# Attention and MLP on one core: last whole weight pieces decoded into PSUM, unit 3 finished ahead of unit 4, step 14's product ahead of step 16

## The chip, the core and the metric

The kernel runs on one core of a Trainium2 chip. The metric is the device time of one execution in microseconds. Its engines work side by side, each through its own queue in order: TensorE (PE, and PEld for its weight loads), VectorE (DVE), ScalarE (ACT), GpSimd (POOL) and SyncE (SP, which issues DMAs). The kernel's program text is ordered by a scheduler in its first part and by hand afterwards, as told below.

## The reference

Attention over 8 batches, 8 heads, 576 positions and 64 elements a head, in fp32, and an MLP on its 4608 x 512 result:

```python
q_d = q.reshape(B, H, Sd, factor, D).mean(axis=3)
...
out_d = sm_attn(q_d, k_d, v_d)
out_up = np.repeat(out_d, factor, axis=2)
mask = np.abs(pos[:, None] - pos[None, :]) < factor
scores = scale * np.matmul(q, k.transpose(0, 1, 3, 2))
scores = np.where(mask, scores, -1000000000.0)
...
out_local = np.matmul(attn, v)
return (out_up + out_local).astype(np.float32)
...
h = x @ w_in
g = np.maximum(h, 0.0) + alpha * np.minimum(h, 0.0)
return (g @ w_out).astype(np.float32)
```

So there is a full attention over 144 averaged positions (factor 4), a local one over seven neighbours, their sum x, and then x (512) to 2048 hidden elements and back to 512.

## The kernel before

**The MLP and its steps.** The 4608 tokens are 18 chunks of 256. A chunk takes 8 steps (NP), each for 256 of the hidden elements, so there are 144 steps. For step s, `hidden` (L771) computes h by 24 matmuls; `slopes` (L782 to L786, ACT) makes the two products whose maximum is the activation; `larger` (L794, DVE, from step EARLY = 12; POOL before) takes the maximum t; `split` (ACT L799, POOL L72) writes t as gh plus gl; `product` (L828) adds 12 matmuls into the chunk's output tiles o; after a chunk's last step `finish` (L834, ACT) copies o out and SP sends it. Each fp32 operand is split in a high and a low part, and a product is high by high, high by low and low by high: xh with wih and wil, xl with wih; gh with woh and wol, gl with woh.

**The weights.** They come as raw fp32 words and are decoded on the chip by `make` (L174 to L226): magnitude (ACT L196), reach (DVE L200, L201), bits (DVE L205, L206), upper (ACT L211 or L215, writes wih or woh) and lower (DVE L219 or L223, writes wil or wol). Pieces fp = 0 to 4 of each matrix are done whole, 1024 elements in each partition, in a ring of two SBUF buffers (temp); pieces 5 to 7 in blocks of 512 in two PSUM banks, "q" and "l".

**The attention.** `down` computes the averaged attention of two heads (qkT L264, s L277, dnb L281, pT L301, pv L311, od L316). `local` computes the local one in units of 192 tokens, three a batch: unit u's scores by a multiply (qk, L608) and a reduction (ls, L612) for three groups of neighbours and two halves, a softmax (L621 to L638), the weighted sums (first L660, weigh L664, gather L667 into the accumulator lb; the far neighbours on POOL, L644), and last (L670), which writes x. PE then transposes x (`flip`, L676, tile xp), DVE adds the averaged attention (`join`, L688, tile xf), and `place` splits xf in xh (ACT L702) and xl (POOL L72). Chunk 2 (steps 16 to 23) needs unit 3's two joins, xf3_0 and xf3_1; chunk 3 (steps 24 to 31) needs unit 4 and the first part of unit 5. Until the chunk's xh and xl are there, its first step can't run.

**What sets the order.** Every piece is an event with a time in steps: `hidden` of step s at s - 1.95, `product` at s + 0.6; a unit's pieces are spread from begin[u] to begin[u + 1], where UNITS gives the first ones; its flips and joins stand at times relative to the next unit's (`before 0`, `before 1`, `own`). The events are sorted. Those before time LISTED = 14 are handed to a scheduler that may reorder them on each engine; those from 14 on are taken as listed (L983 to L990). An engine's queue runs in order, so a row that waits holds up all behind it.

Buffers that matter: both joins of a unit write the one "xf" buffer, which steps before 12 also use for sh; the multiplies of a unit use two "prod" buffers; there are two "pp" buffers for POOL's far products. The banks "q" and "l" hold the decode's blocks, and later a unit's scaled q (qp) and its accumulator.

## Time and profile before

| what | value |
|---|---|
| median of 3 runs | 986.85 us (985.21 to 992.86) |
| the profiled execution | 989.45 us, of which its span 987.6 us |
| busy, share of the span: PE / DVE / ACT / POOL | 96% / 84% / 56% / 51% |
| TensorE's mean granted clock | 0.977 |
| 190 to 204 us: PE busy, clock | 7.64 of 14.00 us, 0.63 |
| 204 to 252 us: PE busy, DVE busy | 47.34 and 43.00 of 48.00 us |
| 600 to 700 us: PE busy, DVE busy | 99.81 and 91.10 of 100 us |

Rows of the timeline give start, duration, engine, line, operation and operands (out<-in), the tile shape and a count of rows taken together; a bracket is the idle time of the engine just before, with the row that ended it. Matmuls overlap at their ends, so a row's start-to-start distance, and not its duration, is its price. Groups of rows add a mean in ns.

### The profile page before, as it was taken

Reading aid. Unit: us, or ns where it says so; the run is one execution under the profiler, and the core shown is the slowest. Engines: PE = TensorE matmul, PEld = TensorE weight load, DVE = VectorE, ACT = ScalarE, POOL = GpSimd, SP = SyncE. Lnnn points to the kernel's source line nnn. Section 1 sums busy time; section 2 is a strip of 40 time slices with the busy share of each in tenths; the row PEclk is TensorE's granted clock in tenths of the full one; section 3 lists DMA queues with packets and bytes.
Section 4 is the critical chain, followed back from the end, with each engine's and each line's share of the span. In section 5 each row is a group of like instructions: output and inputs, shape, how many; then the busy total and the mean of one; then the engine's idle time right before and its main releaser. Section 6 shows DMA issues by size and latency. Waiting matters only on the chain.

```text
span 987.6 us, 17973 instructions
## 1 busy us (share of the span) xinstructions
PE 944.3 (96%) x6402; PEld 844.3 (85%) x6402; DVE 826.4 (84%) x1336; ACT 557.4 (56%) x1483; POOL 508.2 (51%) x624
## 2 busy tenths in 40 slices
PE   5977999799999999999999999999999999999998
PEld 4856887599889998889988899998899989989997
DVE  7799978989888898998989889899898889997111
ACT  4667676355656564655555555555646564444442
POOL 2063886557566545655546455555466633323221
PEclk9966999899999999999999999999999999999999
DMA  8935743123433323242312332322333311310000
GB/s 200 229 136 174 251 131 108 55 81 97 129 112 101 94 84 100 88 138 73 127 59 93 102 121 72 122 79 84 115 102 99 119 47 56 102 33 22 1 22 22
DMA packets 63197, 98.28 MB, mean 100 GB/s; under 512 B 23556, under 2 KB 28932, under 8 KB 63108
## 3 DMA queue, kind: packets, MB, share of 16 engines
q1 hardware_dynamic: 62916, 96.88, 32.5%
q8 instruction: 50, 0.82, 0.3%
q10 hardware_dynamic: 192, 0.26, 0.1%
q14 instruction: 39, 0.32, 0.1%
HBM read 87.67 MB, written 9.44 MB: 98 GB/s over the span
## 4 chain that ended last, share of the span: by engine, by line
PE 81%; DVE 12%; ACT 2%; issue 2%; SPq 1%; POOL 1%; DMA 1%; DVEq 0%; ACTq 0%; POOLq 0%
PE o L828 36%; PE h L771 36%; PE s L277 2%; PE pv L311 2%; PE xp L676 1%; DVE lb L667 1%; PE pT L301 1%; DVE temp L205 1%; DVE temp L206 1%; DVE pv L664 1%; PE fs L462 1%; DVE qk L608 1%; SPq L410 1%; DVE temp L200 1%; DVE wil L219 1%
## 5 line engine op out<-in xcount | busy, mean ns | idle before, releaser
L72 POOL TENSOR_TENSOR gl<-t,gh 128x512 fp32r<-128x512 f32 x144 | 186.3, 1293 | 344.4 <-ACT gh L799 330.9
L782 ACT ACTIVATE t<-h,slope 128x256 f32<-128x256 f32 x288 | 136.4, 474 | 136.1 <-PE h L771 106.4
L771 PE MATMUL h<-xh,wih 128*128 128x256 f32 x1152 | 188.4, 285 | 9.1 <-ACT xh L702 3.5
L828 PE MATMUL o<-woh,gh 128*128 128x512 f32 x576 | 192.5, 404 | 2.7 <-ACT gh L799 1.2
L828 PE MATMUL o<-wol,gh 128*128 128x512 f32 x576 | 185.7, 393 | 0.0
L828 PE MATMUL o<-woh,gl 128*128 128x512 f32 x576 | 185.4, 393 | 0.0
L771 PE MATMUL h<-xl,wih 128*128 128x256 f32 x1152 | 180.2, 279 | 0.9 <-POOL xl L72 0.9
L771 PEld LDWEIGHTS h<-xh,wih 128*128 128x128 f32 x1152 | 163.3, 190 | 20.5 <-ACT sh L784 3.8
L771 PE MATMUL h<-xh,wil 128*128 128x256 f32 x1152 | 180.6, 279 | 0.0
L794 DVE TENSOR_TENSOR t<-h,t 128x512 f32<-128x512 f32 x132 | 90.6, 686 | 94.7 <-ACT h L786 92.2
L75 POOL TENSOR_TENSOR ld<-ld 72x256 f32<-72x256 f32 x168 | 132.5, 791 | 68.2 <-DMA ld<-in_q 64.8
L799 ACT CAST gh<-t 128x512 fp32r<-128x512 f32 x144 | 89.3, 620 | 134.8 <-DVE t L794 101.7
L771 PEld LDWEIGHTS h<-xh,wil 128*128 128x128 f32 x1152 | 155.2, 190 | 0.3
L771 PEld LDWEIGHTS h<-xl,wih 128*128 128x128 f32 x1152 | 154.2, 189 | 1.2 <-POOL xl L72 1.1
L612 DVE TENSOR_REDUCE ls<-qk 128x12 f32<-128x768 f32 (+1 forms) x126 | 136.1, 1082 | 2.9
L828 PEld LDWEIGHTS o<-woh,gl 128*128 128x128 f32 x576 | 108.0, 188 | 24.1
L828 PEld LDWEIGHTS o<-wol,gh 128*128 128x128 f32 x576 | 108.0, 188 | 23.1 <-DVE temp L206 0.2
L667 DVE TENSOR_TENSOR lb<-lb,pv 128x384 f32<-128x384 f32 x202 | 113.9, 564 | 5.7
L786 ACT ACTIVATE h<-h,sign 128x256 f32<-128x256 f32 x264 | 116.0, 439 | 0.0
L828 PEld LDWEIGHTS o<-woh,gh 128*128 128x128 f32 x576 | 99.1, 188 | 19.3 <-issue 2.8
L664 DVE TENSOR_TENSOR pv<-v,lb 128x1152 f32<-128x1152 f32 x84 | 93.6, 1114 | 2.6
L608 DVE TENSOR_TENSOR qk<-k,qp 128x768 f32<-128x768 f32 (+1 forms) x78 | 83.8, 1076 | 2.0 <-ACT qp L602 2.0
(151 smaller groups left out, 1149.2 us busy)
## 6 DMA issues: line engine op xcount, KB each, us to landing
k<-in_k SPq DMA_DIRECT2D x41, 384.0 KB
v<-in_v SPq DMA_DIRECT2D x41, 384.0 KB
out<-sg SPq DMA_DIRECT2D x140, 64.0 KB
raw<-in_moe_w_in SPq DMA_DIRECT2D x16, 512.0 KB
raw<-in_moe_w_out SPq DMA_DIRECT2D x16, 512.0 KB
ld<-in_q SPq DMA_DIRECT2D x56, 144.0 KB
ld<-in_k SPq DMA_DIRECT2D x56, 144.0 KB
ld<-in_v SPq DMA_DIRECT2D x56, 144.0 KB
```

What stands on the lines that cost most here:

```text
L72: nc.gpsimd.tensor_tensor(o, a, b, op=ALU.subtract)
L75: nc.gpsimd.tensor_tensor(o, a, b, op=ALU.add)
L608: nc.vector.tensor_tensor(st["pr"][:, :nd], window(tiles[u, "k"], half, d0, nd), st["qp", half].unsqueeze(1).to_broadcast([128, nd, 2, 192 ...
L612: nc.vector.tensor_reduce(out=st["s"][:, half, d0:d0 + nd, :].rearrange("p a b -> p (a b)"), in_=st["pr"][:, :nd].rearrange("p a h (t d) - ...
L664: nc.vector.tensor_tensor(st["pr"][:, :nd], window4(tiles[u, "v"], half, d0, nd), prob(half, d0, nd), op=ALU.mult)
L667: nc.vector.tensor_tensor(st["acc"], st["acc"], st["pr"][:, i], op=ALU.add)
L771: nc.tensor.matmul(ph[:, j], w[:, m, 128 * o:128 * o + 128], x[:, m, :], start=(i == 0), stop=(i == 11))
L782: nc.scalar.activation(t[:, j], hs[st][:, j], AF.Copy, scale=slope[:, f:f + 1])
L786: nc.scalar.activation(other[:, j], hs[st][:, j], AF.Copy, scale=sign[:, f:f + 1])
L794: nc.vector.tensor_tensor(gs[st], hs.pop(st), gs[st], op=ALU.max)
L799: nc.scalar.copy(gh, t)
L828: nc.tensor.matmul(outs[c][m], g[:, j, 128 * m:128 * m + 128], wo[w][n][:, o, :], start=(f == 0 and i == 0), stop=(f == NF - 1 and i == 2))
```

## The change

Three things are changed. First, in the last whole piece of each matrix (fp = 4) the second instruction of `bits` writes its result in two halves into the PSUM banks "q" and "l" (tiles whole040, whole041, whole140, whole141), and `upper` and `lower` read the halves from there. Second, units 4 to 7 begin later (UNITS), unit 3's flips and joins are put at the beginning of unit 4 (JOINS), its second join gets a buffer of the "pp" kind, unit 4's first multiply is issued after unit 3's last x, and unit 5's "own" join is listed earlier. Third, `product` of step 14 is listed at 14.035 instead of 14.6, and `hidden` of step 16 at 14.4 instead of 14.05.

```diff
--- before.py
+++ after.py
@@ -41,13 +41,14 @@
 N_EARLY = 5
 FIRST = (-1.3, 0.3, 3.4, 6.5)
 T0_DEC, D_DEC = 0.5, 0.56
-UNITS = {3: 7.5, 4: 12.2, 5: 17.4, 6: 22.7, 7: 28.0}
+UNITS = {3: 7.5, 4: 14.0, 5: 18.5, 6: 23.2, 7: 28.2}
 U_STEP = 5.92
 EARLY = 12
 BY_HALF = (5, 9, 13, 17, 21)
 BEHIND = {(1, 0): ((0, 2), (0, 2)), (1, 1): ((1, 4), (0, 5)), (1, 2): ((1, 5), (1, 5))}
 FAR = {3: 2, 4: 2, 5: 2, 6: 2}
 LISTED = 14
+JOINS = (0.04, 0.06)
 
 
 @with_exitstack
@@ -203,24 +204,39 @@
         def bits():
             t, hi, lo = st["t"], st["raw"][:, :, :, 1], st["raw"][:, :, :, 0]
             nc.vector.scalar_tensor_tensor(t, hi, -0x40000000, t, op0=ALU.bitwise_and, op1=ALU.bitwise_or)
-            nc.vector.scalar_tensor_tensor(t, lo, 29, t, op0=ALU.logical_shift_right, op1=ALU.bitwise_or)
+            if c is None and fp == N_EARLY - 1:
+                st["t"] = []
+                for i in range(2):
+                    m = bank("ql"[i], f"whole{which}{fp}{i}").bitcast(I32).rearrange("p (k a) -> p k a", k=k // 2)
+                    part_of = slice(i * k // 2, i * k // 2 + k // 2)
+                    nc.vector.scalar_tensor_tensor(m, lo[:, part_of], 29, t[:, part_of],
+                                                   op0=ALU.logical_shift_right, op1=ALU.bitwise_or)
+                    st["t"].append((part_of, m))
+            else:
+                nc.vector.scalar_tensor_tensor(t, lo, 29, t, op0=ALU.logical_shift_right, op1=ALU.bitwise_or)
+                st["t"] = [(slice(0, k), t)]
+
+        def row_of(i):
+            return next(m[:, i - s.start:i - s.start + 1] for s, m in st["t"] if s.start <= i < s.stop)
 
         def upper():
             weight_tiles(which, n)
             if which == 0:
-                nc.scalar.copy(part(0, 0), f32(st["t"]))
+                for part_of, m in st["t"]:
+                    nc.scalar.copy(part(0, 0)[:, part_of], f32(m))
             else:
                 for i, c in enumerate(cs):
                     sg = sign[:, 2 * fp + c:2 * fp + c + 1]
-                    nc.scalar.activation(part(0, c), f32(st["t"][:, i:i + 1]), AF.Copy, scale=sg)
+                    nc.scalar.activation(part(0, c), f32(row_of(i)), AF.Copy, scale=sg)
 
         def lower():
             if which == 0:
-                nc.vector.tensor_tensor(part(1, 0), f32(st["t"]), f32(part(0, 0)), op=ALU.subtract)
+                for part_of, m in st["t"]:
+                    nc.vector.tensor_tensor(part(1, 0)[:, part_of], f32(m), f32(part(0, 0)[:, part_of]), op=ALU.subtract)
             else:
                 for i, c in enumerate(cs):
                     sg = sign[:, 2 * fp + c:2 * fp + c + 1]
-                    nc.vector.scalar_tensor_tensor(part(1, c), f32(st["t"][:, i:i + 1]), sg, f32(part(0, c)),
+                    nc.vector.scalar_tensor_tensor(part(1, c), f32(row_of(i)), sg, f32(part(0, c)),
                                                    op0=ALU.mult, op1=ALU.subtract)
 
         return magnitude, reach, bits, upper, lower
@@ -539,7 +555,7 @@
         return load_pair, load_windows, pair
 
 
-    tiles = {}
+    tiles, ended = {}, {}
 
     def unit_base(u):
         return (u // 3) * H * HEAD + 6 * (u % 3) * D
@@ -605,8 +621,9 @@
             if "s" not in st:
                 st["s"] = late.tile([128, 2, 7, 6], F32, tag="ls", name=f"ls{u}")
             st["pr"] = late.tile([128, 3, 2, 192], F32, tag="prod", bufs=PB, name=f"qk{u}_{half}{d0}")
-            nc.vector.tensor_tensor(st["pr"][:, :nd], window(tiles[u, "k"], half, d0, nd),
-                                    st["qp", half].unsqueeze(1).to_broadcast([128, nd, 2, 192]), op=ALU.mult)
+            with tc.issue_after(ended[3].ins) if (u, half, d0) == (4, 0, 0) else nullcontext():
+                nc.vector.tensor_tensor(st["pr"][:, :nd], window(tiles[u, "k"], half, d0, nd),
+                                        st["qp", half].unsqueeze(1).to_broadcast([128, nd, 2, 192]), op=ALU.mult)
 
         def total(half, d0, nd):
             nc.vector.tensor_reduce(
@@ -667,7 +684,7 @@
             nc.vector.tensor_tensor(st["acc"], st["acc"], st["pr"][:, i], op=ALU.add)
 
         def last(half):
-            nc.vector.tensor_tensor(st["x"][:, 3 * half:3 * half + 3].rearrange("p t h d -> p h t d"), st["acc"], st["far", half], op=ALU.add)
+            ended[u] = nc.vector.tensor_tensor(st["x"][:, 3 * half:3 * half + 3].rearrange("p t h d -> p h t d"), st["acc"], st["far", half], op=ALU.add)
 
         def flip(i):
             j0, nt = groups[i]
@@ -679,7 +696,11 @@
             j0, nt = groups[i]
             odv = od[b].rearrange("p a (s g) -> p a s g", g=9)
             tp = st.pop(("tp", i))
-            xf = late.tile([128, 512], F32, tag="xf", name=f"xf{u}_{i}")[:, :128 * nt]
+            if (u, i) == (3, 1):
+                xf = late.tile([128, 2, 3, 64], F32, tag="pp", name=f"xf{u}_{i}", bufs=2)
+                xf = xf.rearrange("p h t d -> p (h t d)")[:, :128 * nt]
+            else:
+                xf = late.tile([128, 512], F32, tag="xf", name=f"xf{u}_{i}")[:, :128 * nt]
             xf = st["xf", i] = xf.rearrange("p (a t s) -> p a t s", a=4, s=32)
             for par in range(2):
                 pos = [(18 * par + 6 * jj + j) // 4 for j in range(j0, j0 + nt)]
@@ -724,7 +745,9 @@
         scores[0][4:4] = [(None, "before 0", 1.3)]
         if by_half:
             items = scores[0] + [(shift, (halves[0],), 0.5), (None, "before 1", 1.0), (weights, (halves[0],), 0.8)] + sums[0]
-            items += scores[1] + [(shift, (halves[1],), 0.5), (None, "own", 1.3), (weights, (halves[1],), 0.8)] + sums[1]
+            rest_of = scores[1] + [(shift, (halves[1],), 0.5), (weights, (halves[1],), 0.8)] + sums[1]
+            rest_of.insert(4 if u == 5 else 7, (None, "own", 1.3))
+            items += rest_of
         else:
             items = scores[0] + scores[1] + [(shift, halves, 0.8), (None, "before 1", 1.0), (weights, halves, 1.2)]
             items += sums[0] + sums[1]
@@ -898,11 +921,11 @@
     late = ctx.enter_context(tc.tile_pool(name="late", bufs=1))
 
     for s in range(NS):
-        at(s - 1.95, hidden, s)
+        at(14.4 if s == 2 * NP else s - 1.95, hidden, s)
         at(s - 1.45, slopes, s)
         at(s - 1.15, larger, s)
         at(s - 1.0, split, s)
-        at(s + 0.6, product, s)
+        at(14.035 if s == 14 else s + 0.6, product, s)
         if s % NP == NP - 1:
             at(s + 1.02, finish if s + 1 < NS else finish_last, s // NP)
 
@@ -946,12 +969,15 @@
         if put and u - 1 in BY_HALF:
             flip_at(u - 1, 1, begin[u] + 0.3, flip)
             put(1, when["before 0"])
+        elif put and u == 4:
+            for i in range(2):
+                flip_at(u - 1, i, begin[u] + 0.02 + 0.01 * i, flip)
+                put(i, begin[u] + JOINS[i])
         elif put:
             flip_at(u - 1, 0, begin[u] + 0.3, flip)
             put(0, when["before 0"])
-            t = when["before 0"] + 0.25 if u == 4 else when["before 1"]
-            flip_at(u - 1, 1, max(begin[u] + 0.31, t - 0.6), flip)
-            put(1, t)
+            flip_at(u - 1, 1, max(begin[u] + 0.31, when["before 1"] - 0.6), flip)
+            put(1, when["before 1"])
         put, flip = mine
```

The lines of the changed kernel are 15 to 23 further down (L828 is L851 there). Three places show what moves. Names end in a number of the tile's instance; o1 is chunk 1's output, xp3_0 and xp3_1 the flips of unit 3, s2_0 and qkT2_0 belong to the averaged attention of batch 2.

PE around step 16, before, from the last rows of step 13's product:

```order
L828 MATMUL o1_0_1836<-woh2_914,gl13_2118 128x512
L828 MATMUL o1_1_1837<-woh2_914,gl13_2118 128x512
L676 MATMUL xp3_0_2165<-ident_75,x3_2004 128x128
L676 MATMUL xp3_1_2192<-ident_75,x3_2004 128x128 x2
L264 MATMUL qkT2_0_2244<-ident_75,s2q2_0_1985 128x72 x2
L264 MATMUL qkT2_0_2244<-ident_75,s2k2_0_2069 128x72 x2
L771 MATMUL h16_2286<-xh2_1759,wih0_73 128x256 x4
L771 MATMUL h16_2286<-xh2_1759,wil0_74 128x256 x4
L771 MATMUL h16_2286<-xl2_1760,wih0_73 128x256 x4
L771 MATMUL h16_2286<-xh2_1759,wih0_73 128x256 x4
L771 MATMUL h16_2286<-xh2_1759,wil0_74 128x256 x4
L771 MATMUL h16_2286<-xl2_1760,wih0_73 128x256 x4
```

and now, the end of that product and what follows it:

```order
L851 MATMUL o1_0_1842<-woh2_922,gl13_2109 128x512
L851 MATMUL o1_1_1843<-woh2_922,gl13_2109 128x512
L693 MATMUL xp3_0_2257<-ident_75,x3_2094 128x128 x4
L693 MATMUL xp3_1_2262<-ident_75,x3_2094 128x128 x2
L851 MATMUL o1_0_1842<-woh3_1564,gh14_2176 128x512
L851 MATMUL o1_1_1843<-woh3_1564,gh14_2176 128x512
```

then eight more rows of step 14's product, and:

```order
L851 MATMUL o1_0_1842<-woh3_1564,gl14_2177 128x512
L851 MATMUL o1_1_1843<-woh3_1564,gl14_2177 128x512
L293 MATMUL s2_0_2293<-kd2_0_2241,qd32_100 96x144 x3
L794 MATMUL h16_2303<-xh2_1766,wih0_73 128x256 x4
L794 MATMUL h16_2303<-xh2_1766,wil0_74 128x256 x4
L794 MATMUL h16_2303<-xl2_1767,wih0_73 128x256 x4
```

Step 14's product and s2_0, which stood behind h16, now stand between unit 3's flips and h16; qkT2_0 is issued further up.

DVE around unit 3's last x (x3, second half), before:

```order
L664 TENSOR_TENSOR pv3_14_2115<-v3_1733,lb3_1757 128x384
L608 TENSOR_TENSOR qk4_00_2149<-k4_1932,qp4_0_2095 128x1152
L667 TENSOR_TENSOR lb3_1757<-lb3_1757,pv3_14_2115 128x384
L794 TENSOR_TENSOR t15_2251<-h15_2203,t15_2251 128x512
L612 TENSOR_REDUCE ls4_2148<-qk4_00_2149 128x18
L670 TENSOR_TENSOR x3_2004<-lb3_1757,pv6_3_1_2020 128x2x3x64
L608 TENSOR_TENSOR qk4_03_2190<-k4_1932,qp4_0_2095 128x768
L608 TENSOR_TENSOR qk4_05_2241<-k4_1932,qp4_0_2095 128x768
L688 TENSOR_TENSOR xf3_0_2228<-xp3_0_2165,od1_1025 128x4x4x16
L688 TENSOR_TENSOR xf3_0_2228<-xp3_0_2165,od1_1025 128x2x4x16 x2
L612 TENSOR_REDUCE ls4_2148<-qk4_03_2190 128x12
L612 TENSOR_REDUCE ls4_2148<-qk4_05_2241 128x12
```

and now:

```order
L681 TENSOR_TENSOR pv3_14_2237<-v3_1741,lb3_1764 128x384
L684 TENSOR_TENSOR lb3_1764<-lb3_1764,pv3_14_2237 128x384
L687 TENSOR_TENSOR x3_2094<-lb3_1764,pv6_3_1_2101 128x2x3x64
L625 TENSOR_TENSOR qk4_00_2255<-k4_2010,qp4_0_2214 128x1152
L817 TENSOR_TENSOR t15_2220<-h15_2182,t15_2220 128x512
L709 TENSOR_TENSOR xf3_0_2277<-xp3_0_2257,od1_1033 128x4x4x16
L709 TENSOR_TENSOR xf3_0_2277<-xp3_0_2257,od1_1033 128x2x4x16 x2
L709 TENSOR_TENSOR xf3_1_2284<-xp3_1_2262,od1_1033 128x2x4x16 x2
L629 TENSOR_REDUCE ls4_2254<-qk4_00_2255 128x18
L625 TENSOR_TENSOR qk4_03_2328<-k4_2010,qp4_0_2214 128x768
L629 TENSOR_REDUCE ls4_2254<-qk4_03_2328 128x12
L297 TENSOR_REDUCE dnb2_0_2340<-s2_0_2293 96x3
```

Unit 3's x and both joins have moved ahead of unit 4's scores (qk4, ls4); of these, four multiplies and four reductions now stand behind step 16's maximum t16, which follows the last row shown.

PE around steps 6 to 8, before, from within step 4's product (gh4, gl4):

```order
L828 MATMUL o0_0_1139<-woh2_914,gh4_1328 128x512
L828 MATMUL o0_1_1140<-woh2_914,gh4_1328 128x512
L828 MATMUL o0_0_1139<-wol2_915,gh4_1328 128x512
L828 MATMUL o0_1_1140<-wol2_915,gh4_1328 128x512
L828 MATMUL o0_0_1139<-woh2_914,gl4_1329 128x512
L828 MATMUL o0_1_1140<-woh2_914,gl4_1329 128x512
L301 MATMUL pT1_1_0_1548<-ident_75,dp1_1_1466 72x96 x2
L771 MATMUL h7_1514<-xh0_107,wih3_1283 128x256 x2
L301 MATMUL pT1_1_1_1552<-ident_75,dp1_1_1466 72x96 x3
L771 MATMUL h7_1514<-xh0_107,wih3_1283 128x256 x2
L771 MATMUL h7_1514<-xh0_107,wil3_1284 128x256 x2
L771 MATMUL h8_1595<-xh1_109,wih0_73 128x256 x4
```

and now, from within step 6:

```order
L794 MATMUL h6_1436<-xh0_107,wih3_1291 128x256 x4
L794 MATMUL h6_1436<-xh0_107,wil3_1292 128x256 x4
L794 MATMUL h6_1436<-xl0_108,wih3_1291 128x256 x4
L794 MATMUL h7_1522<-xh0_107,wih3_1291 128x256 x2
L794 MATMUL h8_1603<-xh1_109,wih0_73 128x256 x4
L794 MATMUL h8_1603<-xh1_109,wil0_74 128x256 x4
L794 MATMUL h8_1603<-xl1_110,wih0_73 128x256 x4
```

Step 4's product has moved ahead of step 6, so that step 8's first group follows step 6's last with two rows of step 7 between.

## Prediction

> **What bounds the kernel now.** I read the engines' shares and the 40 slices of the page first, to see which engine is never idle and where it is.
>
> ```profile
> PE 944.3 (96%) x6402; PEld 844.3 (85%) x6402; DVE 826.4 (84%) x1336; ACT 557.4 (56%) x1483; POOL 508.2 (51%) x624
> PE   5977999799999999999999999999999999999998
> ...
> DVE  7799978989888898998989889899898889997111
> ```
>
> TensorE is full except in slices 1, 3, 4 and 8 (of 24.7 us each, the last one 173 to 198 us) and the end. A change that works in the first quarter can only win what PE loses there, or lose something new. The profiled execution took 989.45 us (span 987.6 and 1.85 around it); the three timed runs have a median of 986.85. My sum is made on the profiled execution and the difference is then taken off the median.
>
> Next, PE's timeline around step 16 (start, duration, operation, count; the bracket is idle time ahead and what ended it).
>
> ```profile
> 188.35 0.62 PE L828 MATMUL o<-woh,gl 128*128 128x512 f32 x2
> 190.54 0.55 PE L676 MATMUL xp<-ident,x 128*128 128x128 f32 x3 [1.57 <-DVE x L670]
> 193.45 0.47 PE L264 MATMUL qkT<-ident,s2q 72*128 72x72 f32 x2 [2.36 <-DVE xf L688]
> ...
> 197.62 1.22 PE L771 MATMUL h<-xh,wih 128*128 128x256 f32 x4 [3.45 <-ACT xh L702]
> ```
>
> and the chain that ended last from there on (start, duration, work):
>
> ```profile
> 197.62 5.07 PE h L771 x24
> 202.69 0.73 PE s L277 x6
> 203.42 2.76 PE o L828 x12
> 206.18 2.73 PE h L771 x24
> ```
>
> One product (12 o matmuls) takes 2.76 us, one hidden step (24 h matmuls) 2.73. After step 13's product (188.35 + 0.62 = 188.97) PE waits 1.57 + 2.36 + 3.45 = 7.38 us for unit 3's tokens: x, the flip, the join, the split in xh and xl. Then h16 itself takes 5.07, 2.34 more than h17 with the same matmuls. So step 16 loses 7.38 + 2.34 = 9.7 us, by far the largest loss in the run that this change could reach. This is the DVE order ahead of it:
>
> ```profile
> 186.16 1.34 DVE L608 TENSOR_TENSOR qk<-k,qp 128x1152 f32<-128x1152 f32 x1
> 187.43 0.56 DVE L667 TENSOR_TENSOR lb<-lb,pv 128x384 f32<-128x384 f32 x1
> 188.07 0.69 DVE L794 TENSOR_TENSOR t<-h,t 128x512 f32<-128x512 f32 x1
> 188.68 1.34 DVE L612 TENSOR_REDUCE ls<-qk 128x18 f32<-128x1152 f32 x1
> 189.94 0.55 DVE L670 TENSOR_TENSOR x<-lb,pv 128x384 f32<-128x384 f32 x1
> ...
> 192.13 1.17 DVE L688 TENSOR_TENSOR xf<-xp,od 128x256 f32<-128x256 f32 x3
> ...
> 196.46 0.66 DVE L688 TENSOR_TENSOR xf<-xp,od 128x128 f32<-128x128 f32 x2 [0.17 <-POOL xl L72]
> ```
>
> Three instructions that belong to unit 4 or to step 15 (1.34 + 0.69 + 1.34 = 3.4 us) stand ahead of unit 3's last x, others ahead of the two joins; the second join also waits for POOL's xl, because both joins use one buffer.
>
> **Part one: unit 3 first, product 14 as cover.** In the changed order x follows the last sum directly, so it ends about 3.4 us earlier, near 187, before the product of step 13 is over: the 1.57 goes. Behind the flips (0.75) PE now has product 14 (2.76) and s2_0 (0.73) before h16 wants xh: 4.2 us of cover. In that time DVE does both joins (1.17 + 0.66), and ACT and POOL these:
>
> ```profile
> 193.33 0.62 ACT L702 CAST xh<-xf 128x512 fp32r<-128x512 f32 x1 [2.33 <-DVE xf L688]
> 195.16 1.26 POOL L72 TENSOR_TENSOR xl<-xf,xh 128x512 fp32r<-128x512 f32 x1
> 198.01 0.73 POOL L72 TENSOR_TENSOR xl<-xf,xh 128x256 fp32r<-128x256 f32 x1
> ```
>
> With E the end of product 13: flip to E + 0.7, first join to E + 1.9, xh to E + 2.5, both xl to E + 4.5 at best and E + 4.8 with one 72x256 add of POOL between. h16 starts at E + 4.2 and needs xl two groups (0.91) later, E + 5.1. So no wait, or up to 0.7: I take 0.3. Won here: 9.7 - 0.3 = **9.4 us**. If the cover were gone the loss would be the old one.
>
> **Part two: the decode in PSUM.** It removes the slow forms of these rows:
>
> ```profile
> 95.27 1.47 DVE L206 SCALAR_TENSOR_TENSOR temp<-raw,temp 128x1024 int32<-128x1024 int32 x1
> ...
> 101.60 2.21 DVE L206 SCALAR_TENSOR_TENSOR temp<-raw,temp 128x1024 int32<-128x1024 int32 x1
> 103.74 4.41 DVE L219 TENSOR_TENSOR wil<-temp,wih 128x1024 fp32r<-128x1024 f32 x1
> ...
> 109.27 2.97 DVE L223 SCALAR_TENSOR_TENSOR wol<-temp,sign,woh 128x512 fp32r<-128x512 f32 x2
> ...
> 114.47 0.67 DVE L219 TENSOR_TENSOR wil<-temp,wih 128x512 fp32r<-128x512 f32 x1
> ```
>
> The row at 114.47 is the same subtraction from PSUM for half the size. With eight halves at 0.67 the four whole operations (2.21 + 4.41 + 2.97 and the earlier combine of 1.47, 11.1 in all) cost 5.4 to 6.7, so DVE saves about 5. But the halves now sit in the two banks into which ACT writes the next pieces' magnitudes; in the order these stand behind step 2's second sh, and DVE's reach of those blocks behind the last wol. DVE then idles there for about as long as it saved. I count nothing for x, and a possible loss of as much as it saved, about 4.6, for the range.
>
> The scheduler also moves PE rows: step 8's first group now comes two rows after step 6's last, without step 4's product between, and must wait until ACT has emptied step 6's h.
>
> ```profile
> 126.10 0.62 PE L771 MATMUL h<-xl,wih 128*128 128x256 f32 x4
> ...
> 130.86 0.51 PE L771 MATMUL h<-xh,wih 128*128 128x256 f32 x2 [0.70 <-ACT wih L211]
> 130.68 0.51 ACT L784 ACTIVATE sh<-h,gain 128x256 f32<-128x256 f32 x1
> ```
>
> Before, h6 ended at 126.6 and its emptying at 131.2, 4.6 us later, with decode work between; four ACT rows alone take about 1.75 (h16 ends at 202.69, and the row at 204.47 below starts on ACT's last, so 1.78 at most). With two h rows (0.23) as cover the wait is 1.5 to 4.4; I take 2.1, near the lower end with one 0.62 us cast ahead, against the 0.70 of before: **1.4 us lost**, bounds -0.7 (no wait at all) and 3.7.
>
> **Part three: what DVE owes afterwards.** Unit 4's scores stood ahead of step 16's maximum, in the time of PE's stall; most of them now stand behind it. Their small reductions are of the kind of this group,
>
> ```profile
> L612 DVE TENSOR_REDUCE ls<-qk 128x12 f32<-128x768 f32 x4 | 3.8, 947 | 0.1
> ```
>
> (a group of DVE's rows from 204 to 252: busy time, mean ns of one, idle before) and in time order
>
> ```profile
> 204.47 0.69 DVE L794 TENSOR_TENSOR t<-h,t 128x512 f32<-128x512 f32 x1 [2.39 <-ACT h L786]
> ...
> 207.84 0.32 DVE L633 TENSOR_REDUCE lb<-lex 128x12 f32<-128x84 f32 x1 [1.68 <-ACT lex L628]
> ...
> 246.81 1.01 DVE L688 TENSOR_TENSOR xf<-xp,od 128x192 f32<-128x192 f32 x3
> ```
>
> From that maximum to the join that chunk 3 (step 24) needs there were 43.35 us, 1.68 of them a wait: 41.7. Behind the maximum come four multiplies and four reductions of unit 4 (three pairs of 0.95 + 0.95, a multiply being as long as its reduction, and one of 1.34 + 1.34, as at 186.16 and 188.68: 8.4); away go dnb2_0 (about 0.6), and behind the join one pair of unit 5 (1.9) with four small rows (0.2 each): 41.7 + 8.4 - 3.3 = 46.8. PE's side:
>
> ```profile
> 250.16 0.73 PE L771 MATMUL h<-xh,wih 128*128 128x256 f32 x4
> ...
> 252.21 0.74 PE L771 MATMUL h<-xl,wih 128*128 128x256 f32 x4 [0.87 <-POOL xl L72]
> ```
>
> h16 to h24 was 250.16 - 197.62 = 52.5; without the slow groups (2.34), product 14 (2.76) and s2_0 (0.73), which now lie ahead, 46.7. With S the start of h16: the maximum starts at S + 2.73 + 1.78 (202.69 to 204.47), the join ends at S + 51.3, h24 can start some 0.9 later, S + 52.2, and PE is there at S + 46.7. So PE waits **5.5 us** between step 20 and step 24, in pieces at the flips of units 4 and 5 and at h24, where it waited 0.87 before: 4.6 lost. Bounds: 0.87 gained if DVE's idle rests hold it all, 6.3 lost if the 1.68 stays too. I stay at 4.6 because 40.17 of the stretch's 43.50 us were already busy:
>
> ```profile
> 204.40:247.90 43.50, 43.50 (x304) 39.26 (x303) 40.17 (x74) 24.89 (x74) 31.44 (x40) 1.00 0.31 91
> ```
>
> (columns: length, then busy PE, PEld, DVE, ACT, POOL; clock; DMA share; GB/s). A second price lies behind it: unit 6's last x and flip.
>
> ```profile
> 289.82 0.55 DVE L670 TENSOR_TENSOR x<-lb,pv 128x384 f32<-128x384 f32 x1
> ...
> 292.30 0.60 PE L676 MATMUL xp<-ident,x 128*128 128x128 f32 x4
> ```
>
> The slack there was 1.9; DVE's debt is met by then about as far as PE's gain has shrunk, so I count nothing more. POOL's xl for chunk 3 now stands ahead of two multiplies of 1.62 instead of behind them, which is why I let h24 start 0.9 after the join.
>
> **Sum.** 9.4 - 1.4 - 4.6 = 3.4 us gained: 989.45 - 3.4 = 986.05 on the profiled execution, 986.85 - 3.4 = **983.4** on the median.
>
> **The rivals.**
>
> A: DVE keeps up. Idle time that the groups hide (POOL contention, say) shrinks as PE's demand comes later, and h24 waits for nothing. For: DVE's share over the whole span is 84%, not 96. Against: the stretch's 40.17 of 43.50. Gain 9.4 - 1.4 + 0.9 = 8.9: **978.0**. Chance 0.17.
>
> B: the new wait falls in one piece, and PE pays twice. The wait of 3.45 ahead of h16 was followed by 2.34 us of slow groups, that of 1.25 at step 1's product by none:
>
> ```profile
> 103.43 0.50 PE L828 MATMUL o<-woh,gh 128*128 128x512 f32 x1 [1.25 <-ACT gh L799]
> 103.77 0.40 PE L828 MATMUL o<-wol,gh 128*128 128x512 f32 x1
> ```
>
> A single wait of 5.5 at h24 would add 2.34: gain 1.1, **985.8**. Against: the order puts two flips ahead of h24 that depend on the same DVE chain, so pieces of 1 to 3 are likelier. Chance 0.13. The Trainium skill, "TensorE: Matmul & The Clock Gate", Part 1, says that the array falls to half rate after an idle window of about 3.4 us; the 3.45 here agrees, and by that rule waits in pieces stay free, as the forecast has them.
>
> C: the change doesn't do what it says, because unit 3's x isn't earlier. If the decode really costs DVE 4.6 us more, x ends near 191.7 instead of 187.1; PE reaches the flip at 188.97 + 1.4 = 190.4 and waits 1.3, the joins shift with it and the cover of 4.2 stays; unit 4's debt begins later by as much. Gain 3.4 - 1.3 - some 1.3 at the next wait = 0.8: **986.0**. For: slices 3 to 5 of DVE (49 to 123 us) are at nine tenths or more. Against: the slices behind them, up to 190 us, are at seven to nine, so it can catch up. Chance 0.16.
>
> D, slower: the last weight pieces come late to PE. The pieces that ACT can only start when the banks are free are for step 5 on, and all later ones queue behind them. Price: h8's wait at its upper bound (3.7) and 4.6 us at the first product that needs the last output piece, which already waited 0.67 for ACT's woh. Gain 9.4 - 3.7 - 4.6 - 4.6 = -3.5: **990.3**. It decides once the loss before step 16 exceeds 9.4 - 4.6 = 4.8. Against: between 135 and 185 us PE hardly waits for weights now. Chance 0.10.
>
> **How the numbers follow.** Forecast 0.44, A 0.17, B 0.13, C 0.16, D 0.10. The forecast's own bounds run from a gain of 9.4 + 0.7 - 4.6 = 5.5 to 9.4 - 1.4 - 6.3 = 1.7. The range takes in A below and B and C above, and leaves out D and A's upper corner: 977.5 to 988.5. One per cent, 9.9 us, is about what a measurement of this kernel can tell from no change; faster by more than that (below 977.0) needs A with no wait at h8: 0.10. Slower by more (above 996.7) needs D with a second fault: 0.04. Within: 0.86.
>
> **What would show it.** Right: no bracket over 1 us at the flips of unit 3 and at h16, and a clock of 1.00 there; wil and wol rows of about 0.7 with whole in their operands; a wait of 1 to 3 at h8; new brackets that sum to 4 to 6 at the flips of units 4 and 5 and at h24, with DVE nearly without idle time from 200 to 245. Wrong: PE full from 190 to 260 (A), one bracket of 5 and slow groups behind it (B), the old 1.57 at unit 3's flip (C), or brackets of some us released by ACT wih or woh between 125 and 165 (D).

## The result, and the profile after

The changed kernel is slower: 990.92 us (median of 20 runs, 988.93 to 997.11) against 985.83 (20 runs, 984.22 to 992.86); the ratio is 1.005, 95% interval 1.0036 to 1.0064. The forecast was 983.4 in a range of 977.5 to 988.5.

First, where the clock of a comparison starts. The first profile of before took 989.45 us, 3.6 more than its median. A second profile of the same program (e4, below) took 986.63. PE's last rows of step 1 and of the whole run, first profile of before:

```profile
92.83 0.62 PE L771 MATMUL h<-xl,wih 128*128 128x256 f32 x4
...
983.08 0.40 PE L828 MATMUL o<-woh,gl 128*128 128x512 f32 x1
```

second profile of before:

```profile
89.38 0.62 PE L771 MATMUL h<-xl,wih 128*128 128x256 f32 x4
...
980.26 0.40 PE L828 MATMUL o<-woh,gl 128*128 128x512 f32 x1
```

and the changed kernel:

```profile
90.88 0.62 PE L794 MATMUL h<-xl,wih 128*128 128x256 f32 x4
...
985.19 0.40 PE L851 MATMUL o<-woh,gl 128*128 128x512 f32 x1
```

Step 1 ended at 93.45, 90.00 and 91.50. From there to the end it is 890.0, 890.7 and 894.1 us. What lies ahead of step 1's end varies by some 5 us from one profile to the next (step 1 ends between 89.9 and 94.9 us over all of them); what lies behind it repeats within 0.7 in the two profiles of before. So places are compared below by their distance from step 1's end, each read as start plus duration of the last row of that step, and times by the medians of runs beside runs of before. In the tables h17 is the end of step 17's `hidden`, product 13 the end of step 13's `product`.

| distance from the end of h1, us | product 13 | h17 | h24 | h26 | h32 | h84 | end |
|---|---|---|---|---|---|---|---|
| before | 95.5 | 115.5 | 160.9 | 174.0 | 211.5 | 533.1 | 890.0 |
| before again (e4) | 95.9 | 115.5 | 160.9 | 174.0 | 211.8 | 533.5 | 890.7 |
| changed | 98.6 | 108.6 | 158.7 | 176.0 | 213.8 | 537.0 | 894.1 |
| difference to the mean of before | +2.9 | -6.9 | -2.2 | +2.0 | +2.1 | +3.7 | +3.7 |

The row of differences says where time went: 2.9 us are lost ahead of step 16, 9.8 are won at it, 4.6 are paid back up to step 24 and 4.2 more in the two steps behind, and 1.6 go between steps 32 and 84.

Step 16 in the changed kernel (PE's timeline):

```profile
189.49 0.62 PE L851 MATMUL o<-woh,gl 128*128 128x512 f32 x2
189.95 0.81 PE L693 MATMUL xp<-ident,x 128*128 128x128 f32 x6
190.53 0.70 PE L851 MATMUL o<-woh,gh 128*128 128x512 f32 x2
...
193.38 0.90 PE L293 MATMUL s<-kd,qd 128*96 128x144 f32 x6
194.01 0.73 PE L794 MATMUL h<-xh,wih 128*128 128x256 f32 x4
194.58 0.62 PE L794 MATMUL h<-xh,wil 128*128 128x256 f32 x4
195.13 0.74 PE L794 MATMUL h<-xl,wih 128*128 128x256 f32 x4
```

No bracket is left: flip, product 14, s2_0 and h16 follow each other, and the groups start 0.45 to 0.58 apart. The waits are elsewhere now. Ahead of step 16:

```profile
132.31 0.74 PE L794 MATMUL h<-xh,wih 128*128 128x256 f32 x4 [1.63 <-ACT sh L807]
...
150.79 0.74 PE L794 MATMUL h<-xh,wih 128*128 128x256 f32 x4 [0.77 <-ACT sh L807]
158.39 0.74 PE L794 MATMUL h<-xh,wih 128*128 128x256 f32 x4 [1.31 <-ACT sh L807]
164.83 0.50 PE L851 MATMUL o<-woh,gh 128*128 128x512 f32 x1 [0.72 <-ACT sg L857]
```

4.43 us where before had 0.70, 0.67 and 0.73. And behind it:

```profile
207.04 0.50 PE L851 MATMUL o<-woh,gh 128*128 128x512 f32 x1 [0.80 <-ACT sg L857]
...
223.74 0.33 PE L693 MATMUL xp<-ident,x 128*128 128x128 f32 x1 [0.52 <-DVE x L687]
228.11 0.44 PE L693 MATMUL xp<-ident,x 128*128 128x128 f32 x2 [1.30 <-ACT dp L303]
...
241.61 0.52 PE L693 MATMUL xp<-ident,x 128*128 128x128 f32 x3 [0.80 <-DVE x L687]
242.53 0.71 PE L327 MATMUL pv<-th,s2v 72*64 72x144 f32 x8 [0.40 <-ACT kd L288]
...
258.26 0.63 PE L693 MATMUL xp<-ident,x 128*128 128x128 f32 x3 [2.61 <-DVE x L687]
...
264.25 0.41 PE L317 MATMUL pT<-ident,dp 96*72 96x96 f32 x3 [0.83 <-DVE xf L709]
```

From h17 to h24 all brackets sum to 4.3 us, where before had 0.9. Flips of units 4 and 5 wait for x three times, the last time 2.61 us, and behind that one the clock falls to a half (length, busy PE, PEld, DVE, ACT, POOL; clock; DMA share; GB/s):

```profile
258.60:262.00 3.40, 3.40 (x10) 2.75 (x9) 3.37 (x4) 2.66 (x8) 1.62 (x4) 0.50 0.57 220
204.00:252.00 48.00, 43.70 (x297) 38.24 (x297) 44.94 (x82) 22.93 (x65) 33.69 (x45) 1.00 0.34 106
```

From 204 to 252 PE was busy 47.34 of 48 us before and is 43.70 now, while DVE rose from 43.00 to 44.94.

### The profile page after: what moved, and what is told of

It reads as the page before. It is cut to its first block, busy times and chain, and to the rows that moved or that the text cites. A ratio compares the mean times of both kernels' runs of the same rounds, so it can differ in the third digit from the quotient of the medians.

```text
span 989.7 us, 17982 instructions
## 1 busy us (share of the span) xinstructions
PE 945.2 (96%) x6402; PEld 843.4 (85%) x6402; DVE 822.5 (83%) x1339; ACT 559.6 (57%) x1484; POOL 511.3 (52%) x624
## 4 chain that ended last, share of the span: by engine, by line
PE 72%; DVE 13%; POOL 4%; DMA 3%; ACT 3%; issue 2%; SPq 2%; DVEq 0%; ACTq 0%; POOLq 0%
PE o L851 33%; PE h L794 32%; DVE lb L684 2%; DVE qk L625 2%; DVE pv L681 2%; DVE ls L629 2%; PE s L293 2%; SPq L426 1%; PE pv L327 1%; POOL ld L76 1%; DMA ld<-in_q 1%; PE xp L693 1%; DVE t L817 1%; DMA fv<-in_v 1%; POOL gl L73 1%
## 5 line engine op out<-in xcount | busy, mean ns | idle before, releaser
L851 PE MATMUL o<-woh,gh 128*128 128x512 f32 x576 | 192.4, 404 | 2.5 <-ACT sg L857 1.5
L851 PE MATMUL o<-wol,gh 128*128 128x512 f32 x576 | 186.6, 394 | 0.0
L851 PE MATMUL o<-woh,gl 128*128 128x512 f32 x576 | 186.1, 394 | 0.0
L76 POOL TENSOR_TENSOR ld<-ld 72x256 f32<-72x256 f32 x168 | 135.1, 805 | 67.0 <-DMA ld<-in_q 59.5
L851 PEld LDWEIGHTS o<-woh,gl 128*128 128x128 f32 x576 | 108.2, 188 | 24.2 <-issue 0.2
L851 PEld LDWEIGHTS o<-wol,gh 128*128 128x128 f32 x576 | 108.4, 189 | 23.5 <-DVE wol L239 0.4
L851 PEld LDWEIGHTS o<-woh,gh 128*128 128x128 f32 x576 | 99.6, 189 | 18.5 <-ACT sg L857 2.2
```

The lines of the kernel that those rows point to most:

```text
L76: nc.gpsimd.tensor_tensor(o, a, b, op=ALU.add)
L851: nc.tensor.matmul(outs[c][m], g[:, j, 128 * m:128 * m + 128], wo[w][n][:, o, :], start=(f == 0 and i == 0), stop=(f == NF - 1 and i == 2))
```

## The experiments

Times are medians beside runs of before on the same chip; ratios have 95% intervals. The distances are from the end of h1, as above.

| kernel | time / before | ratio | product 13 | h17 | h26 | end |
|---|---|---|---|---|---|---|
| e1 decode alone | 992.34 / 987.54 | 1.0051 (1.0031 to 1.0072) | 99.7 | 119.2 | 177.6 | 894.3 |
| e5 decode, first matrix | 989.67 / 986.76 | 1.0024 (1.0005 to 1.0043) | 95.7 | 115.4 | 173.9 | 890.3 |
| e6 decode, second matrix | 992.17 / 986.76 | 1.0049 (1.0024 to 1.0074) | 99.6 | 119.5 | 178.0 | 894.6 |
| e9 second matrix, banks d | 982.58 / 987.62 | 0.9958 (0.9934 to 0.9982) | 92.1 | 109.6 | 168.1 | 884.7 |
| e3 product 14 alone | 986.88 / 987.54 | 0.9999 (0.9979 to 1.0019) | 95.5 | 111.9 | 173.9 | 890.3 |
| e2 changed, old decode | 988.72 / 987.54 | 1.001 (0.9989 to 1.003) | 94.8 | 105.4 | 172.8 | 891.3 |
| e7 e2, maximum later | 987.07 / 986.76 | 1.0002 (0.9977 to 1.0028) | 95.6 | 106.3 | 171.8 | 889.9 |
| e8 e7, flip later | 989.18 / 986.76 | 1.0025 (1.0005 to 1.0044) | 95.6 | 106.3 | 174.5 | 892.8 |
| e10 e7, units 7 on back | 984.93 / 987.62 | 0.9976 (0.9954 to 0.9998) | 95.3 | 105.8 | 171.4 | 887.7 |
| e11 e10, maximum still later | 986.51 / 987.62 | 0.9979 (0.9959 to 1.0) | 95.2 | 105.7 | 170.6 | 886.9 |
| e13 changed, banks d | 986.70 / 986.13 | 0.9999 (0.9979 to 1.0019) | 92.1 | 102.6 | 170.1 | 888.2 |
| e12 e11 and banks d | 984.02 / 986.13 | 0.998 (0.9962 to 0.9999) | 93.1 | 103.6 | 168.5 | 885.6 |
| e14 e2, lighter DVE | 983.85 / 986.48 | 0.9956 (0.9932 to 0.998) | 95.5 | 106.1 | 168.7 | 886.8 |
| e15 before, lighter DVE | 986.10 / 986.48 | 0.9993 (0.997 to 1.0016) | 95.3 | 115.5 | 173.4 | 890.1 |

**e1, the decode alone.** before.py with the changed `bits`, `upper` and `lower`.

> The kernel before with the PSUM decode of the last whole pieces alone; units, joins and the product stay. Theory one (the decode loses time before step 16): in the changed kernel the waits of PE between 125 and 165 us sum to 4.4 us against 2.1 before, and product 13 ended 3.1 us later counted from the end of h1; so this kernel is 2 to 4 us slower than before, with brackets of 1 to 2 us at h8 and near 150 to 160 released by ACT sh, and the stall at step 16 stays at 6 to 8 us. Rival (all loss is made behind step 16 by VectorE's debt): the same time as before within 1 us, since the decode's gain and loss cancel.

Slower by 4.8 us (3.9 counted from h1): the decode alone costs as much as the whole change. PE's brackets are nearly those of the changed kernel (1.63, 1.02, 1.31, 0.73), the stall at step 16 stays. The rival fell.

**e2, everything but the decode.**

> The changed kernel with the old decode; it keeps the unit times, the joins of unit 3 and product 14 ahead of step 16. Theory one with theory two (what is won at step 16, 9 to 10 us, is paid back by waits of PE for unit 4's and 5's x before step 26, 8 to 9 us): no wait at h8, step 16 without a stall, brackets that sum to 6 to 9 us between 220 and 262 us, and a time within 1.5 us of before, 3 to 4 us better than the changed kernel. Rival (the loss before step 16 comes from the move of unit 4 and not from the decode): 4 to 5 us slower than before, as the changed kernel is.

The wait at h8 is that of before (0.74), product 13 is in time, 10.1 us are won at step 17 and 8.9 of them are gone at h26. The time is that of before within its interval: the two other parts together neither win nor lose more than 0.3%.

**e3, product 14 alone.**

```diff
-        at(s - 1.95, hidden, s)
+        at(14.4 if s == 2 * NP else s - 1.95, hidden, s)
...
-        at(s + 0.6, product, s)
+        at(14.035 if s == 14 else s + 0.6, product, s)
```

> The kernel before with product 14 and step 16's first matmuls moved alone; VectorE's order is that of before. PE puts product 14 (2.76 us) into the wait for unit 3's x, the flip follows it about 1.2 us later than before, so step 16 wins about 1.5 us and VectorE owes nothing new. Theory two (only work moved behind step 16's maximum is paid back): 1 to 2.5 us faster than before, with at most 1 us of new brackets before step 26. Rival (VectorE has no slack at all up to step 32, any gain of PE there is paid back): the same as before within 0.5 us, with new brackets at xp5_1 or xp6_0 as long as the gain.

h17 came 3.6 us earlier, more than expected, and h26 only 0.2: even with DVE's order unchanged nothing was left. Here the rival was right, though by other waits than it named (1.57 for ACT's sg, 1.17 for a join of unit 4, 1.06 instead of 0.87 at h24): a PE that is early behind step 16 meets the other engines at their old times.

**e4, before once more.**

> The kernel before once more, for a second profile. The first one took 989.45 us where the median of twenty is 985.83. Theory (the first profile lost 2 to 4 us before step 2, in rows that are the same in both kernels): here h1 ends near 90 us instead of 93.45, and everything behind it is earlier by the same amount, with the same 7.4 us of stall at step 16. Rival (the spread is made later, along the whole span): h1 ends near 93 us and the time differs elsewhere.

h1 ended 3.5 us earlier, at 90.00, and the end came 2.8 earlier, with 7.5 us of stall at step 16.

**e5 and e6, the decode of one matrix each.** One condition in `bits`, here against e1:

```diff
-            if c is None and fp == N_EARLY - 1:
+            if which == 0 and c is None and fp == N_EARLY - 1:
```

(`which == 1` in e6).

> The kernel before with the PSUM decode of the last whole piece of the first matrix alone. Decode in PSUM of both cost about 4.8 us. Theory one a (it is the second matrix's halves that cost: DVE must wait for ACT's woh, 1.72 us in the changed kernel, while both banks are held, and the two blocks that follow leave phase): at most 1.5 us slower than before. Rival (any whole piece in PSUM makes the scheduler move step 4's product and the blocks, whichever matrix it is of): 3 to 5 us slower, with the wait at h8.

> The kernel before with the PSUM decode of the last whole piece of the second matrix alone. Theory one a: 3 to 5 us slower than before, with brackets released by ACT sh at h8 and between 150 and 162 us, the last wol about 5 us later counted from the end of h1 (72 instead of 66.5). Rival (it is the first matrix's halves): within 1 us of before.

The second matrix's halves carry all of it: e6 ends 4.2 us behind before, with the last wol at 71.9 us behind h1 against 66.3. e5 has the distances of before to 0.3 us from product 13 on, so nothing behind h1 explains its ratio of 1.0024; its one profile reached h1 late, at 94.25, but where its other runs lost time is not shown. ACT's magnitudes of the first two blocks show what goes with the loss. In e6 (ACT's timeline):

```profile
103.80 0.69 ACT L229 ACTIVATE woh<-whole,sign 128x512 fp32r<-128x512 f32 x1 [2.83 <-DVE whole L211]
104.98 0.69 ACT L229 ACTIVATE woh<-whole,sign 128x512 fp32r<-128x512 f32 x1
...
107.51 1.22 ACT L196 ACTIVATE temp<-raw 128x512 f32<-128x512 f32 x2
```

with h1 at 90.00: 17.5 us behind it. In before, with h1 at 93.45, 3.2 behind it:

```profile
96.62 1.21 ACT L196 ACTIVATE temp<-raw 128x512 f32<-128x512 f32 x2
```

In the changed kernel, e1 and e6 the magnitudes start 1.0 to 1.3 us behind the last read of the halves that lie in q and l (the second wol).

**e9, the same halves in other banks.** The d banks serve the averaged attention and the flips. Against e6 one line differs:

```diff
-                    m = bank("ql"[i], f"whole{which}{fp}{i}").bitcast(I32).rearrange("p (k a) -> p k a", k=k // 2)
+                    m = bank("d", f"whole{which}{fp}{i}").bitcast(I32).rearrange("p (k a) -> p k a", k=k // 2)
```

> The kernel before with the last whole piece of the second matrix decoded into PSUM, but into the two banks of the averaged attention (d) and not into q and l, where the later blocks' magnitudes go. Counted from the end of h1, the kernel with q and l ended 4.2 us later than before, with the first block's magnitude at 17.5 us instead of 3.2. Theory one b (holding q and l costs it: the block chain starts only behind wol): the magnitudes come at 3 to 11 us, the last wol at 64 to 68 and not at 72, the end within 1.5 us of before. Rival (the halves themselves, or the order that the scheduler finds, cost it): the last wol at 70 to 73 and the end 3 to 5 us later than before.

Expected was no loss; it became a gain of 5.0 us, the best of all kernels here that do all the work. The magnitudes come ahead of the halves again, 2.3 us behind h1 (89.85):

```profile
92.13 1.22 ACT L196 ACTIVATE temp<-raw 128x512 f32<-128x512 f32 x2
...
97.14 0.69 ACT L229 ACTIVATE woh<-whole,sign 128x512 fp32r<-128x512 f32 x1 [0.84 <-DVE whole L211]
```

and PE has no bracket between 95 and 184 us. The stall at step 16 is still there (2.30 and 3.57), but all behind it is 5.5 to 5.9 us earlier, and nothing of that is paid back up to the end: 3.6 us are won up to product 13 and 2.3 at step 16's stall. So with the halves out of banks q and l the loss is gone.

The whole gain isn't the work of the new forms, though. Of VectorE's rows from the second matrix's combine to its wol, before spends 2.21, 4.41 and 2.97 us and e9 2.65, 1.22 and 1.40. The largest part of the 4.3 us saved, 3.2, is in the first matrix's subtraction, which e9 leaves as it was (DVE's timelines of e9 and, for the piece ahead of that one, of before):

```profile
98.73 1.22 DVE L234 TENSOR_TENSOR wil<-temp,wih 128x1024 fp32r<-128x1024 f32 x1
```

```profile
84.79 1.22 DVE L219 TENSOR_TENSOR wil<-temp,wih 128x1024 fp32r<-128x1024 f32 x1
```

It takes 1.16 to 1.22 us in all four earlier pieces of before as well, and 4.41 only in the last one; the section on the hardware says what runs beside it. The edit also made the scheduler find another order ahead of step 8 (e6, e1 and the changed kernel share one, with step 4's product ahead of step 6; e9, as before, has most of that product behind step 6). What the bank costs and what that order costs was not measured apart.

**e7 and e8, DVE's wait filled, then the flip moved.** In e2 DVE stood idle for 3.71 us ahead of the maximum of step 16 (3.05 in the changed kernel). e7 lists it later, behind one more pair of unit 4's scores; e8 also lists unit 5's second flip behind product 23.

```diff
-        at(s - 1.15, larger, s)
-        at(s - 1.0, split, s)
+        at(15.2 if s == 2 * NP else s - 1.15, larger, s)
+        at(15.35 if s == 2 * NP else s - 1.0, split, s)
...
-            flip_at(u - 1, 1, begin[u] + 0.3, flip)
+            when_flipped[u - 1, 1] = begin[u] + 0.3
+            at(23.75 if u == 6 else begin[u] + 0.3, flip, 1)
```

> The changed kernel with the old decode, and step 16's maximum listed at 15.2 (its split at 15.35), so that DVE does one pair of unit 4's scores in the 3 us in which it waited for h16. Theory two (DVE's debt is what PE waits for up to step 26): the wait of DVE for t16 shrinks from 3 to 1 us, x of unit 4 and 5 come 1.5 to 2 us earlier, PE's brackets from 215 to 262 us fall from about 6.8 to 4 to 5 us, and the time is 1.5 to 2.5 us below that of the changed kernel with the old decode, so 0.5 to 1.5 us faster than before. Rival (PE waits because the flips stand too early in its queue, DVE has time): brackets and time as without this edit, 1 us slower than before.

> As the kernel with the maximum later, and unit 5's second flip listed behind product 23 instead of ahead of it (chunk 4 needs it only at step 32). Rival of theory two (the flip stands too early): its wait of 2.6 us and the half clock behind it (1.7 us) go, 3 to 4 us faster than the kernel with the maximum later. Theory two (DVE is the bound as far as unit 6's x): the wait goes there, but a new one comes at unit 6's first flip near 290 us, and the gain is 1.5 us at most.

e7's wait there fell to 1.90; it won about 1 us at h26, less than expected, and its time is that of before. e8 lost 2.7 us more: the flip no longer waits, but the next small matmul does, since the flip holds its bank until DVE has joined it (PE's timeline of e8):

```profile
258.96 0.67 PE L302 MATMUL pT<-ident,dp 96*72 96x96 f32 x3 [4.58 <-DVE xf L694]
```

So the wait moved, as theory two had it, but to another place than it said, and to a loss that neither side had expected.

**e10 and e11, later units back, maximum still later.** UNITS 7 at 28.0 again (e10); then larger at 15.45 and split at 15.6 (e11).

> The kernel with the old decode and the maximum later, with UNITS 7 at 28.0 as before, so that units 8 and on have their old times. From h32 to h84 the kernels with the new unit times took 323.3 us and those with the old ones 321.7. Theory three (the order of small matmuls among the large ones costs it, and it comes from the later units' times alone): 321.7 +- 0.3 here, and the end 1.5 us earlier than in the kernel with the maximum later, 1.5 to 2.5 us faster than before counted from h1. Rival (it comes from what unit 4 to 6 leave behind): 323.3 as there.

> The kernel with units 7 and on back, and step 16's maximum still later (15.45, split 15.6), behind one more multiply of unit 4 (1.34 us) in place of 1.9 us in which DVE waited. Theory two (DVE's debt): x of units 4 and 5 are 1.2 to 1.4 us earlier, the wait at unit 5's second flip falls from 2.4 to about 1 us and the half clock behind it (1.7 us) goes, so h26 ends 2 to 3.5 us earlier than with the maximum at 15.2 and the run is 4 us (3 to 5) faster than before. Rival (bank and ACT waits, not DVE, hold PE from 220 to 262 us): h26 within 0.5 us of the kernel with the maximum at 15.2.

e10 settles theory three: from h32 to h84 it took 321.7 us, as before did, where e7 took 323.3. A shift of 0.2 step in the units from 7 on costs 1.6 us there, with the same 2214 matmuls. The expectation put that to their order alone; but 0.73 to 0.75 us of it is one wait ahead of step 51, which every kernel with the new unit times has and none with the old ones (e7, PE):

```profile
412.19 0.32 PE L265 MATMUL qkT<-ident,s2q 72*128 72x72 f32 x2 [0.75 <-ACT th L306]
```

The other 0.9 us is spread over some fifty steps without a pause, which fits the order of the small matmuls.

e11 won 0.8 us more at h26, not 2 to 3.5: x came earlier, and PE too, so the wait at unit 5's second flip stayed at 2.61. The half clock did go, and that won nothing: the wait behind it grew from 0.85 to 2.43 us (e11, PE):

```profile
251.33 0.55 PE L678 MATMUL xp<-ident,x 128*128 128x128 f32 x3 [2.61 <-DVE x L672]
...
257.32 0.41 PE L302 MATMUL pT<-ident,dp 96*72 96x96 f32 x3 [2.43 <-DVE xf L694]
```

From the flip to the row that waits for its join it is 5.99 us in e10, at a mean clock of 0.72, and 5.99 us in e11, at 1.00 (lengths and columns as above, e10, then e11):

```profile
254.30:260.29 5.99, 5.14 (x18) 3.93 (x19) 5.96 (x10) 4.65 (x12) 2.91 (x5) 0.72 0.40 131
```

```profile
251.33:257.32 5.99, 3.56 (x18) 2.80 (x19) 5.96 (x10) 4.64 (x12) 3.07 (x5) 1.00 0.40 131
```

DVE is busy for 5.96 us of both: it goes without a pause from x through four rows of unit 6's scores and a maximum to the join, and PE waits for that, at whichever clock.

**e13 and e12, the banks in the changed kernel.** e13 is the changed kernel with e9's decode; e12 adds e11's edits.

> The changed kernel with one edit: the halves of the second matrix's last whole piece go to the two banks d, and the first matrix's piece is decoded as before. Theory one b (holding q and l is the whole loss ahead of step 16): no wait at h8, product 13 ends 92 us behind h1 instead of 98.6, and what the reorder does is as in the changed kernel with the old decode (1.0 us slower than before), so the end is near 886 us behind h1, 8 us less than the changed kernel's 894.1, and the run 3 to 5 us faster than before. Rival (the parts of the change hinder each other, VectorE being in debt already): the end at 889 to 892, the same as before or slower.

> The same with units 7 and on at their old times and step 16's maximum at 15.45 (split 15.6). If the parts add: 3.5 us (those two edits beside the old decode, counted from h1) and 5.5 us (the decode in the d banks) less than before, so the end at 881 to 883 us behind h1 and the run 7 to 9 us faster than before (977 to 980), with the wait of 2.6 us at unit 5's second flip still there. If VectorE's debt eats the decode's gain: the end at 885 to 887, as with either one alone.

e13 undoes 5.9 of the changed kernel's distance (888.2 for 894.1), not 8: at h17 it is 7.0 us ahead of e9, at h26 2.0 behind, and its time is that of before, where 3 to 5 us less were expected. e12 ends at 885.6 and is 2.1 us faster than before, not 7 to 9: no better than e9 with one edit. The parts don't add. One reason shows in the distances: 2.3 of e9's 5.6 us are won at step 16's stall, which the reorder removes by itself.

**e14 and e15, less work on DVE.** Both leave out the eight additions of unit 4's weighted sum.

```diff
         def gather(i):
+            if u == 4:
+                return
```

> The changed kernel with the old decode, leaving out the eight additions of unit 4's weighted sum on DVE (8 x 0.57 = 4.6 us; its x is then wrong in value). Theory two (VectorE's amount of work up to unit 6 is what PE waits for): x of units 4 and 5 come about 4.5 us earlier, the brackets between 215 and 262 us (6.9 us, with 1.7 us of half clock) fall to 2 to 3 us, h26 ends 5 to 6 us earlier than with the additions (167 to 168 us behind h1 instead of 172.8), and the run is 3 to 5 us faster than before. Rival (PE waits for banks, for ACT's dp and for flips that stand too early): brackets as with the additions, h26 at 171 to 173.

> The control: the kernel before leaving out the same eight additions. There PE's only wait behind step 16 is 0.87 us at h24 and 0.5 near 264. Theory two: the stall at step 16 stays, h26 ends at 173 us behind h1 (174.0 with the additions) and the time is within 1 us of before. Rival: DVE's work was a bound here too, h26 2 us earlier or more.

4.1 us at h26 and 4.5 at the end for e14 (5 to 6 were expected at h26), 0.6 and 0.2 for the control. All of e2's brackets from 215 to 250 us are gone; what is left is (e14, PE):

```profile
254.34 0.62 PE L680 MATMUL xp<-ident,x 128*128 128x128 f32 x3 [2.29 <-DVE x L674]
260.32 0.41 PE L302 MATMUL pT<-ident,dp 96*72 96x96 f32 x3 [0.83 <-DVE xf L696]
```

The same 4.6 us of DVE work are worth 4.5 us behind the reorder and nothing in before: VectorE's amount of work is the bound from step 17 to step 26 once PE doesn't stall at step 16. From h17 to h24 e14 takes 45.6 us, as before does; from h24 to h26 it still takes 17.0 for 13.1, since PE comes to unit 5's second flip earlier by as much as x does.

## Why the prediction was wrong

**Step 16: right.** Forecast 9.4 us won; from product 13 to h17 it is 19.6 to 19.9 before and 10.0 now, 9.8 won, and 9.1 to 9.2 in the kernels with the old decode, where h16 waits 0.6 us for xl. In the changed kernel the flips and h16 wait for nothing, so rival C, with its old 1.57 at the flip, fell. The clock was read too coarsely: the prediction put the half clock in before to the wait of 3.45, but the rate fell at 191.79, before that wait began, behind the wait of 1.57 and inside that of 2.36 (before; the last columns are clock, DMA share and GB/s):

```profile
188.97:191.79 2.82, 0.55 (x4) 0.31 (x3) 2.82 (x4) 0.98 (x2) 1.95 (x2) 1.00 0.42 167
191.79:195.20 3.41, 0.71 (x4) 0.53 (x4) 3.41 (x7) 1.47 (x4) 1.13 (x3) 0.50 0.38 115
```

So the 3.45 doesn't bear out a rule by which waits in shorter pieces stay free.

**The decode: the step that failed first.** The prediction wrote "I count nothing for x, and a possible loss of as much as it saved", and took 1.4 us for h8 alone. It cost 2.9 in the changed kernel and 3.9 to 4.2 alone (e1, e6). The prediction had seen that the halves sit in the next blocks' banks, and priced it as DVE time idled against DVE time saved. For DVE that balance held: the rows it named took 6.7 us instead of 11.1, so 4.3 were saved (about 5 forecast), and 3.6 went in two waits (changed kernel, DVE):

```profile
103.51 1.51 DVE L239 SCALAR_TENSOR_TENSOR wol<-whole,sign,woh 128x512 fp32r<-128x512 f32 x2 [1.72 <-ACT woh L230]
106.92 1.30 DVE L201 TENSOR_SCALAR temp<-temp 128x512 f32<-128x512 f32 x2 [1.90 <-ACT temp L197]
```

What it left out is the price for PE, a later start of the whole chain of blocks: magnitude, reach, bits, upper and lower pass between ACT and DVE, each block holds its bank through all five, and two banks are all there is. The first block's magnitude came 14.8 us behind h1 instead of 3.2 (106.25 in the changed kernel), the last wol 4.7 to 5.0 us later, and PE met it as waits for ACT at h8, h11 and h12. At h8 alone 0.9 was lost (1.63 for 0.70), less than the 1.4 that was counted. The late chain is what rival D named, at one chance in ten; but its sign, waits of PE for wih or woh, didn't come: PE waited for sh, the emptying of h. e9, by the one line that gives the halves other banks, turned the loss of 4.2 into a gain of 5.6; that holding the banks costs it, and not the order that the scheduler makes of it, is likely and not shown apart.

**The debt up to h24: right.** Forecast 4.6 us (5.5 of waits for 0.87); from h17 to h24 it is 45.4 before and 50.1 now, and e14 shows that VectorE's work makes it: with 4.6 us less of that work, e2's 50.1 falls to 45.6. That it came out to a tenth is luck: 0.80 of the waits are for ACT's sg, and at h24, where a piece was expected, PE waited 0.22. Rival A, a PE that is full from 190 to 260, fell.

**Behind h24: the step that failed second.** The prediction looked for a second price at unit 6's first flip, found 1.9 us of slack and wrote "I count nothing more". It passed over unit 5's second flip in between. In before that x (DVE) was done at 256.5 and its flip (PE) ran at 257.0:

```profile
255.96 0.56 DVE L670 TENSOR_TENSOR x<-lb,pv 128x384 f32<-128x384 f32 x1
```

```profile
257.00 0.49 PE L676 MATMUL xp<-ident,x 128*128 128x128 f32 x3
```

Half a microsecond of slack, and the work ahead of it on DVE had been made longer. In the changed kernel (DVE):

```profile
199.15 0.69 DVE L817 TENSOR_TENSOR t<-h,t 128x512 f32<-128x512 f32 x1 [3.05 <-ACT h L809]
...
240.92 0.55 DVE L687 TENSOR_TENSOR x<-lb,pv 128x384 f32<-128x384 f32 x1
...
257.65 0.56 DVE L687 TENSOR_TENSOR x<-lb,pv 128x384 f32<-128x384 f32 x1
```

Counted from h1, the maximum of step 16 came 3.4 us earlier than before and this x 3.6 later. From h24 to h26 4.2 us more than before are lost: PE waits 2.61 us for x and then for the join that ends 6.45 us behind x's start. The stretch at half clock between the two adds nothing to that: e11 without it takes 17.25 us from h24 to h26, e10 with it 17.26. The Trainium skill, "TensorE: Matmul & The Clock Gate", Part 1, gives half rate after an idle window of about 3.4 us; here a wait of 2.61 was enough, so rival B's condition was too strict. Its extra price didn't come here, since PE had VectorE to wait for in any case.

**Not in the sum.** The later units' times cost 1.6 us from h32 to h84 (e10), 0.7 of them in one wait; the prediction put nothing for them and gave no reason. And the profile that the sum was made against had lost 3.5 us ahead of h1; taking only the difference off the median kept that out of the forecast.

So the sum would have been 9.8 - 2.9 - 4.6 - 4.2 - 1.6 = -3.5, close to the measured distance (3.7 us later). The largest term is the second failed step, 4.2 us put at nothing, then the decode and the later units, each some 1.5 us more than was counted. The medians differ by 5.1; the other 1.4 us can lie ahead of h1, where runs vary, but no run shows it. Most of what was to show the forecast right came true (no stall at step 16, wil and wol rows of 0.7, a wait at h8, brackets that sum to 4.3 up to h24); the loss was made where nothing had been named to look at.

## What to carry to other kernels

A result put into another memory is paid for by how long it holds its place there: ask which step is next in line for that bank, and price the delay of the whole chain behind it, not only the instruction that got faster. When a stall of the bounding engine goes, the next engine's order decides how much stays; sum that engine's work up to each later point at which the two meet, every one of them, since half a microsecond of slack that is passed over can cost as much as the wait that was priced. Before a row is called slow for its form, look whether the same row is fast elsewhere in the trace. And compare profiles from a common point behind the part that varies by itself.
